# Two more units of a mixture's second product by two Strassen levels, with one set of weight sums

## The chip, the cores and the metric

The kernel runs on one core of one Trainium2 chip. The metric is the device time of one execution in microseconds (us); lower is better. All data are fp32.

## The reference

Linear attention with a decay for each head feeds a mixture of four experts. What is computed, cut to what matters:

```python
# q, k, v: (4, 8, 768, 64); blocks of 64 positions
intra = (qb @ kb.T) * Dmask @ vb
inter = (qb * lam_pow) @ kv_state
kv_state = lam ** 64 * kv_state + (kb * rev_pow).T @ vb
x = attention.transpose(0, 2, 1, 3).reshape(3072, 512)
p = domain_probs / domain_probs.sum(-1)           # (3072, 4)
for e in range(4):                                # w1: (4, 512, 1024), w2: (4, 1024, 512)
    h = maximum(x @ w1[e], 0)
    out += p[:, e:e + 1] * (h @ w2[e])
```

## The kernel before

The 3072 tokens lie in 3 groups g of 1024. A **unit** is one pair (g, e) of group and expert; there are 12. For each unit there is a **first product** (x @ w1, with two Strassen levels: seven outer products M1 to M7, each of seven inner products) and a **second product** (h @ w2). The second product comes in two kinds:

- **One level** (`second_product`, L1071): seven products, each of 4 parts (two token halves by two output halves), each part 4 matmuls of 128x128 by 256. VectorE multiplies each part by the token's gate and adds it to an accumulator (L1089). h is the left operand, so the sums that Strassen needs are formed of h as S sums, and those of w2 as T sums (`prepare_w2`, kept in `w2_sums` in DRAM).
- **Two levels** (`nested_product`, L1370): seven products of seven inner products, 2 matmuls each. w2 is the left operand, in inner operands kept in DRAM (`w2_ops`, made by `prepare_w2_ops` from S sums of w2), and h the right one, with T sums. GpSimd multiplies h by the gate beforehand (`gated`) and forms the inner sums of h (`inner_sums`); VectorE forms the outer sums (`outer_sums`) and adds each inner result to `sums` (seven tiles of the `stage` pool). Results of experts add up there. The result is transposed: group 1's is parked in DRAM, gathered and transposed by VectorE (`first_result`), group 2's is turned at the end.

`NEST` is the index of the first unit of the second kind. Before it is 6: units 0 to 3 are (0, 0) to (0, 3), 4 and 5 are (1, 0) and (1, 1), 6 and 7 are (1, 2) and (1, 3), 8 to 11 are (2, 2), (2, 3), (2, 0), (2, 1). Group 1 so has both kinds: the one-level part of its result goes to DRAM as `partial` and is added on GpSimd when the parked part comes back.

The order is written out by hand. The main loop goes over units `at` and products `i` (7 a unit): an **iteration** does product i of unit `at`'s second product beside product i of unit `at + 1`'s first product. It has 8 **slots** x; slot number is (7 at + i) 8 + x. In each slot a few matmuls are issued, then things from lists: `background` (sums on VectorE), `lately` (attention's VectorE steps), `aside` (GpSimd's gating and inner sums), and `pump`, which starts **chores**. Chores are the steps that prepare weights on GpSimd: load blocks of w1 or w2, form a sum, form one product's inner operands and later store them. `pump` spaces chores by an estimate of GpSimd's time: `tt` adds elements / 480 slots (640 in the two-level stage) to `busy`, and the next chore may begin after PACE times that. A store is queued two slots after the estimated end of its step.

Nearly all DMAs are issued by SyncE (SP in the profile) in program order: a DMA that waits for its data or its buffer holds up all that follow. `feed` loads the next iteration's w1 operands (`ws_in`, 896 KB, two buffers; issued in slot x = 0 of the one-level stage), `feed2` w2 operands two iterations ahead, `feed3` those of the two-level product.

Attention of groups 1 and 2 runs inside the one-level stage, a chunk of 128 tokens at a time: chunk i of group g has its base slot s at BEGIN[g][0] + BEGIN[g][1] i; it loads at s - 10 (`load_more`), and then `turn`, `scores` and `values` follow. Group 2's chunks use a copy of q and k rearranged through DRAM (`across`): 128 small DMAs of 32 KB, 32 for each of the four batches, on the list `pieces`. `trickle` issues one of them in every odd slot; `load_more` first issues all that are left of its batch and earlier ones:

```python
            trickle(sum(b <= where(n)[1] for b, _ in pieces))
            load_across(n)
            load(n, "k")
```

`pair_sums` forms the Strassen sums of two chunks' output on GpSimd and stores them in `x_blocks`; `x_fill` loads them for group 2's (and group 1's) first product at iteration FILL.

Of the kernel before, what the change touches and what calls it, by code (L numbers as in the profile page):

```python
# [12 lines left out]
ALU = mybir.AluOpType  # L13
# [8 lines left out]
def kernel(  # L22
# [30 lines left out]
    nc = tc.nc  # L53
# [47 lines left out]
    def tt(eng, o, a, b, op):  # L101
        eng.tensor_tensor(out=o, in0=a, in1=b, op=op)  # L102
        if eng is nc.gpsimd:
            busy[0] = max(busy[0], now[0]) + math.prod(o.shape[1:]) / (640 if spare else 480)
        else:
            vector(math.prod(o.shape[1:]), PSUM in (a.space, b.space))
# [15 lines left out]
    units = [(g, e) for g in range(NG) for e in ((2, 3, 0, 1) if g == LAST else range(E))]  # L122
    unit_of = {u: x for x, u in enumerate(units)}
    NEST = 2 * E - 2
# [39 lines left out]
    w2_sums = dram.tile([E, 4, P, 2, W], FP32, name="w2_sums")  # L164
# [45 lines left out]
    def inner(eng, what, to, blk, ops, at):  # L210
# [3 lines left out]
        for i, (name, x, y, op) in enumerate(ops):  # L214
            b[name] = s[:, SLOT[name]]
            tt(eng, b[name], b[x], b[y], op)
        store(lambda: (
            nc.sync.dma_start(out=to[:, 0], in_=blk[:, 0, 0:256]),
            nc.sync.dma_start(out=to[:, 1:5], in_=s[:]),
            nc.sync.dma_start(out=to[:, 5:7], in_=blk[:, 1].rearrange("p (a f) -> p a f", a=2)),  # L220
            made.add(what),
        ))

    SLOT = {"S3": 0, "S2": 1, "S1": 2, "S4": 3, "T3": 0, "T2": 1, "T4": 2, "T1": 3}
# [44 lines left out]
    def w2_block(e, uu, i, j):  # L269
        r = uu * W + i * 256  # L270
        return moe_w2[e, r:r + 256, j * DH:(j + 1) * DH].rearrange("(c p) d -> p c d", p=P)

    def prepare_w2(e):
        st = {}

        def block(name, i, j):
            t = stage.tile([P, 2, 2, DH], FP32, name="w2b", tag="st")
            for uu in range(2):
                for c in (slice(0, 1), slice(1, 2)) if e == 0 else (slice(0, 2),):
                    nc.sync.dma_start(out=t[:, uu, c], in_=w2_block(e, uu, i, j)[:, c])  # L280
            st[name] = t

        def total(name, n, a, b, op):
            t = stage.tile([P, 2, 2, DH], FP32, name="w2o", tag="st")
            flat = [x[:].rearrange("p u c d -> p (u c d)") for x in (t, st[a], st[b])]
            halves(*(x[:].rearrange("p u c d -> p u (c d)") for x in (t, st[a], st[b])), op)
            store(lambda: (
                nc.sync.dma_start(out=w2_sums[e, n].rearrange("p u w -> p (u w)"), in_=flat[0]),
                made.add(("w2", e, name)),
            ))  # L290
            st[name] = t

        return [
            lambda: (block("B12", 0, 1), block("B22", 1, 1)), pause(4),
            lambda: block("B11", 0, 0),
            lambda: total("T3", 2, "B22", "B12", ALU.subtract),
            lambda: (block("B21", 1, 0), total("T1", 0, "B12", "B11", ALU.subtract)),
            lambda: total("T2", 1, "B22", "T1", ALU.subtract),
            lambda: total("T4", 3, "B21", "T2", ALU.subtract),
        ]  # L300


# [14 lines left out]
    def prepare_w2_ops(e, eased):  # L317
        st = {}

        def two(name):  # L320
            if eased:
                t = [small(name)[:] for _ in range(2)]
            else:
                t = stage.tile([P, 2, W], FP32, name=name, tag="st")
                t = [t[:, q] for q in range(2)]
            return [x.rearrange("p (c d) -> p c d", c=2) for x in t]

        def block(name, i, j):
            t = st[name] = two("w2b")
            for q in range(2):  # L330
                r = j * W + q * 256
                src = moe_w2[e, r:r + 256, i * DH:(i + 1) * DH]
                nc.sync.dma_start(out=t[q], in_=src.rearrange("(c p) d -> p c d", p=P))

        def total(name, a, b, op):
            t = two("w2o")
            for q in range(2):
                tt(nc.gpsimd, t[q], st[a][q], st[b][q], op)
            st[name] = t

        def ready(m):
            inner_w2(e, m, st[A_OF[m]], two)

        if not eased:
            return weight_steps(block, total, ready)

        def less():
            a, b = st["A11"], st.pop("A21")
            for q in range(2):
                tt(nc.gpsimd, b[q], a[q], b[q], ALU.subtract)  # L350
            st["S3"] = b

        def drop(*names):
            for n in names:
                del st[n]

        return [
            lambda: (block("A21", 1, 0), block("A22", 1, 1)), pause(6),
            lambda: total("S1", "A21", "A22", ALU.add),
            lambda: (ready("M4"), block("A11", 0, 0), drop("A22")), pause(4),  # L360
            less, lambda: ready("M7"), lambda: (ready("M1"), drop("S3")), lambda: ready("M5"),
            lambda: (total("S2", "S1", "A11", ALU.subtract), block("A12", 0, 1)), lambda: ready("M6"),
            lambda: ready("M2"),
            lambda: total("S4", "A12", "S2", ALU.subtract), lambda: ready("M3"),
        ]

    SUM_AT = {"T1": 0, "T2": 1, "T3": 2, "T4": 3}
# [171 lines left out]
    gate_bc = decay[:]  # L539
# [240 lines left out]
    def pair_sums(g, x, o):  # L780

        s = stage.tile([P, 4, 256], FP32, name="to", tag="st")
        (b12, b11), (b22, b21) = ((t[:, 0:256], t[:, 256:512]) for t in o)
        for to, a, b in ((0, b12, b11), (1, b22, s[:, 0]), (2, b22, b12), (3, b21, s[:, 1])):
            tt(nc.gpsimd, s[:, to], a, b, ALU.subtract)
# [3 lines left out]
            nc.sync.dma_start(out=x_blocks[g - 1, :, x, 3:7], in_=s[:]),  # L789
# [4 lines left out]
    BEGIN = {1: (24, 13), 2: (8 * 19, 16)}  # L794
    steps = []

    def attention(g):
# [3 lines left out]

        for i in range(CPG):
# [3 lines left out]
            put(s, lambda n=n: turn(n, ("s0", "s1")))  # L806
            if comes_across(n):
                put(s - 2, lambda n=n: (decayed(n), nat.pop((n, "k"))))
            put(s + (6 if comes_across(n) else 4), lambda n=n: scores(n, ("s0", "s1")))
            put(s + (12 if comes_across(n) else 10), lambda n=n: values(n, ("s0", "s1")))  # L810
            if n == NG * CPG - 1:
                put(s + 17, turn_gates)
        steps.sort(key=lambda s: s[0])

    def forget():
        while lately:
            take(lately, True)
        assert not states
# [5 lines left out]
    hid = {}  # L824
    def operands(key):

        h = hid[key]

        def step():
            t = h["S3"] = h.pop("A21")  # L830
            tt(nc.vector, t[:], h["A11"][:], t[:], ALU.subtract)

        background.append(step)

    def later_operands(g, e, m):

        def step(h, a):
            if m == "M4":
                t = h["S2"] = h.pop("S3")
                tt(nc.vector, t[:], a[:], t[:], ALU.subtract)  # L840
            elif m == "M2":
# [58 lines left out]
    def inner_sums(e, m, behind=False):  # L900
# [6 lines left out]
        def total(name, x, y):  # L907
            while len(blk) < 4:
                take(background if B_OF[m] in SUM_AT else aside, True)
# [843 lines left out]
```

## Time and profile before

| | before |
|---|---|
| time, median of 3 runs | 1161.52 us (1161.19 to 1163.1) |
| the profiled execution: span from first to last instruction | 1164.6 us |
| TensorE (PE) busy | 1149.6 us, 8039 instructions |
| VectorE (DVE) busy | 810.8 us |
| GpSimd (POOL) busy | 748.3 us |
| ScalarE (ACT) busy | 306.2 us |
| granted TensorE clock | 0.998 |
| one-level stage, 90 to 684 us | DMA share 0.80 |
| two-level stage, 684 to 1113 us | DMA share 0.73 |

The page gives the profiled execution no other time than its span. An engine's busy time leaves out DMA issues and waits. PE counts each fp32 matmul as two instructions. In groups of instructions, the columns are busy time, mean ns of one, and idle time before them with what ended it. In stretches, the columns are the stretch, its length, busy time of each engine with its instructions, TensorE's granted clock, DMA share and GB/s. SPq is SyncE's queue. L102 is the helper through which all two-operand steps of VectorE and GpSimd go.

### The profile page before, as it was taken

To read this page: it belongs to the slowest core of one execution; us is meant where nothing else is said; L and a number is where in the kernel's file an instruction comes from. 1 tells how busy PE (TensorE), PEld (TensorE's weight loads), DVE (VectorE), ACT (ScalarE), POOL (GpSimd) and SP (SyncE) were. 2 spreads that over 40 slices of the span, in tenths; PEclk is the share of its full clock that TensorE was granted. 3 is DMA by queue.
4 is the path that set the end of the run, shared out by engine and by line. 5 is a ranking of instruction groups with operands and counts; after the bars stand their busy time and mean duration, and the time that the engine had idled before them with its cause. 6 is when DMAs were issued, how large, how long until landed. Compare 5 with 4: busy or idle time off the path is not lost.

```text
span 1164.6 us, 21683 instructions
## 1 busy us (share of the span) xinstructions
PE 1149.6 (99%) x8039; PEld 997.4 (86%) x8039; DVE 810.8 (70%) x1483; ACT 306.2 (26%) x618; POOL 748.3 (64%) x720
## 2 busy tenths in 40 slices
PE   8899999999999999999999999999999999999998
PEld 7788888888888888888888888888888888888887
DVE  4576896477478757747946775688875677777785
ACT  4312122112201211221221243342343341341232
POOL 2747427456754862243646395897995898995894
PEclk9999999999999999999999999999999999999999
DMA  8883668999999797787969557676668877876542
GB/s 191 213 277 119 182 190 255 311 297 284 314 301 298 258 315 204 205 261 240 291 204 281 187 190 227 213 225 216 212 222 261 244 230 227 277 225 212 172 190 73
DMA packets 291705, 270.63 MB, mean 232 GB/s; under 512 B 139600, under 2 KB 239504, under 8 KB 291600
## 3 DMA queue, kind: packets, MB, share of 16 engines
q1 hardware_dynamic: 278848, 265.36, 74.1%
q10 hardware_dynamic: 12752, 3.89, 1.5%
q8 instruction: 64, 1.05, 0.4%
q14 instruction: 41, 0.34, 0.1%
HBM read 191.55 MB, written 81.82 MB: 235 GB/s over the span
## 4 chain that ended last, share of the span: by engine, by line
PE 93%; DVE 4%; DMA 1%; issue 1%; ACT 0%; ACTq 0%; DVEq 0%
PE pg L1017 39%; PE q L1071 24%; PE pq L1370 19%; PE pM L1473 3%; PE pc L1473 2%; DVE m L102 2%; PE sp L676 1%; PE op L730 1%; DMA ws_in<-w_ops 1%; PE op L748 1%; PE sp L683 1%; DVE sums L102 1%; PE qp L646 1%; PE kp L646 1%; DVE hT L102 0%
## 5 line engine op out<-in xcount | busy, mean ns | idle before, releaser
L1017 PE MATMUL pg<-xs,ws_in 128*128 128x256 f32 x1960 | 472.0, 381 | 2.3 <-DMA ws_in<-w_ops 1.2
L1017 PEld LDWEIGHTS pg<-xs,ws_in 128*128 128x128 f32 x1960 | 369.5, 190 | 56.5 <-DVE m L102 4.6
L102 DVE TENSOR_TENSOR m<-pg,m 128x512 f32<-128x512 f32 x451 | 307.1, 687 | 124.6 <-PE pg L1017 112.8
L1071 PE MATMUL q<-w2t,m 128*128 128x256 f32 x1344 | 318.7, 380 | 0.5 <-DVE m L102 0.5
L1071 PEld LDWEIGHTS q<-w2t,m 128*128 128x128 f32 x1344 | 254.1, 190 | 35.8 <-DVE m L102 1.2
L102 POOL TENSOR_TENSOR m<-m,decay 128x512 f32<-128x512 f32 x96 | 121.0, 1282 | 75.2 <-ACT m L1029 58.0
L1029 ACT ACTIVATE m<-m 128x512 f32<-128x512 f32 x132 | 83.0, 630 | 244.4 <-DVE m L102 241.0
L1370 PE MATMUL pq<-acc,w2t 128*128 128x256 f32 x576 | 141.9, 379 | 0.2 <-DVE sums L102 0.2
L102 DVE TENSOR_TENSOR sums<-pq,sums 128x256 f32<-128x256 f32 x223 | 92.7, 421 | 59.2 <-PE pq L1370 47.8
L1089 DVE SCALAR_TENSOR_TENSOR acc<-q,gate,acc 128x256 f32<-128x256 f32 x136 | 65.4, 481 | 87.5 <-PE q L1071 86.6
L1370 PEld LDWEIGHTS pq<-acc,w2t 128*128 128x128 f32 x576 | 109.2, 190 | 15.7 <-POOL w2o L102 0.5
L102 DVE TENSOR_TENSOR m<-m,m 128x512 f32<-128x512 f32 x136 | 112.9, 830 | 4.2 <-ACT m L1029 4.2
L1025 ACT COPY m<-pg 128x512 f32<-128x512 f32 x88 | 51.5, 585 | 161.7 <-PE pg L1017 158.7
L102 POOL TENSOR_TENSOR acc<-hT,acc 128x512 f32<-128x512 f32 x48 | 61.3, 1276 | 5.2 <-PE pq L1370 1.8
L102 POOL TENSOR_TENSOR to<-xc 128x256 f32<-128x256 f32 x16 | 12.6, 785 | 79.6 <-DVE xc L102 47.1
L102 POOL TENSOR_TENSOR acc<-hT,hT 128x512 f32<-128x512 f32 x48 | 60.7, 1282 | 3.9 <-PE pq L1370 3.9
L1370 PE MATMUL pq<-hT,w2t 128*128 128x256 f32 x240 | 61.6, 379 | 0.0
L102 POOL TENSOR_TENSOR xs<-xs 128x256 f32<-128x256 f32 x40 | 30.4, 761 | 47.0 <-DMA xs<-x_blocks 33.3
L102 POOL TENSOR_TENSOR kn<-kn,decay 128x512 f32<-128x512 f32 x16 | 18.1, 1133 | 63.2 <-PE kp L646 27.6
L949 ACT COPY up<-m 128x512 f32<-128x512 f32 x48 | 27.8, 589 | 101.6 <-DVE m L102 101.4
L881 ACT COPY hp<-m 128x512 f32<-128x512 f32 x72 | 41.6, 589 | 37.5 <-DVE hT L102 20.3
L1370 PEld LDWEIGHTS pq<-hT,w2t 128*128 128x128 f32 x240 | 45.6, 190 | 6.2
(140 smaller groups left out, 1371.0 us busy)
## 6 DMA issues: line engine op xcount, KB each, us to landing
ws_in<-w_ops SPq DMA_DIRECT2D x70, 896.0 KB, 6.9
w2t<-w_ops SPq DMA_DIRECT2D x108, 256.0 KB, 3.7
w2b<-in_moe_w_dram SPq DMA_DIRECT2D x56, 256.0 KB, 6.1
w_ops<-ops SPq DMA_DIRECT2D x28, 512.0 KB, 4.7
w2t<-w_sums SPq DMA_DIRECT2D x48, 256.0 KB, 3.7
w2t<-in_moe_w_dram SPq DMA_DIRECT2D x36, 256.0 KB, 3.9
w_sums<-w2o SPq DMA_DIRECT2D x16, 512.0 KB, 5.4
xs<-x_blocks SPq DMA_DIRECT2D x28, 256.0 KB, 4.5
```

Of the source, the lines that this page charges most:

```text
L102: eng.tensor_tensor(out=o, in0=a, in1=b, op=op)
L646: nc.tensor.transpose(out=x[:, ac * C:(ac + 1) * C], in_=y[:, 2 * ac:2 * ac + 2].rearrange("p r d -> p (r d)"), identity=ident[:],)
L676: nc.tensor.matmul(out=sp[r][half[x], ac * BL:(ac + 1) * BL], lhsT=hc(kT)[half[r], ac, blk[x]], rhs=hc(qT)[half[r], ac, blk[x]], start=(ac ...
L881: nc.scalar.copy(out=there[x][:], in_=blk[at][:])
L949: nc.scalar.copy(out=there[at][:], in_=a[at][:])
L1017: nc.tensor.matmul(out=p[:, j * 256:(j + 1) * 256], lhsT=ws[i][:, j * P:(j + 1) * P], rhs=xs[i], start=(fresh and j == 0), stop=True, skip ...
L1025: nc.scalar.copy(out=new[at][:], in_=p[:])
L1029: nc.scalar.activation(out=new[at][:], in_=new[at][:], func=AF.Relu)
L1071: nc.tensor.matmul(out=p[:, s * DH:(s + 1) * DH], lhsT=h[A_OF[m]][:, c * 256 + s * P:c * 256 + (s + 1) * P], rhs=fed2[g, e, m][uu][:, c], ...
L1089: nc.vector.scalar_tensor_tensor(out=o, in0=x, scalar=w, in1=o, op0=ALU.mult, op1=ALU.add)
L1370: nc.tensor.matmul(out=p[:, 0:256], lhsT=fed3[e, m, x // 2][:, x % 2, c * P:(c + 1) * P], rhs=b[B_OF[i]][:, c * 256:(c + 1) * 256], start= ...
L1473: nc.tensor.matmul(out=p[:, s * 256:(s + 1) * 256], lhsT=a[c][:, f:f + P], rhs=b[:, c, j * 256:(j + 1) * 256], start=(s == 0 and c == 0 an ...
```

## The change

`NEST` becomes 4: group 1's units all take the two-level second product, in the order (1, 2), (1, 3), (1, 0), (1, 1). `partial` goes. The one-level product now takes w2 as the S operand and h as the T operand, so that one set of w2 sums in DRAM (`w2_sums`, S1 to S4) serves both kinds: for experts 2 and 3 `prepare_w2` forms the sums and the inner operands in one pass, for experts 0 and 1 `prepare_w2_ops` later reads the sums back. The T sums of h are formed in the place of operands no longer needed. GpSimd's steps are counted at 640 elements a slot everywhere, with a PACE for each unit. Group 2's attention begins at slot 128 and takes 13 slots a chunk. Gates are turned at slot 12 and broadcast into two tiles of the common pool. The plain blocks of w1 are no longer copied into `w1_ops`: for M1, M2 and M4 `feed` loads three pieces. `pair_sums` uses tiles of the common pool in place of `stage`. The core of the diff:

```diff
-            busy[0] = max(busy[0], now[0]) + math.prod(o.shape[1:]) / (640 if spare else 480)
+            busy[0] = max(busy[0], now[0]) + math.prod(o.shape[1:]) / 640
...
-    units = [(g, e) for g in range(NG) for e in ((2, 3, 0, 1) if g == LAST else range(E))]
+    units = [(g, e) for g in range(NG) for e in ((2, 3, 0, 1) if g else range(E))]
-    NEST = 2 * E - 2
+    NEST = E
...
+        if both:                                   # prepare_w2(e, both=True)
+            return [
+                lambda: block("A11", "A21"), lambda: block("A22"), pause(4),
+                lambda: ready("M1"),
+                lambda: total("S3", "A11", "A21", ALU.subtract), lambda: ready("M7"),
+                lambda: total("S1", "A21", "A22", ALU.add), lambda: ready("M5"),
+                lambda: ready("M4"),
+                lambda: (block("A12"), total("S2", "S1", "A11", ALU.subtract)), lambda: ready("M6"),
+                lambda: ready("M2"),
+                lambda: total("S4", "A12", "S2", ALU.subtract), lambda: ready("M3"),
+            ]
...
+        return [                                   # prepare_w2_ops(e)
+            lambda: fetch(SEQ3[0]), pause(4),
+            *(lambda i=i: (i < 6 and fetch(SEQ3[i + 1]), ready(SEQ3[i])) for i in range(7)),
+        ]
...
-    BEGIN = {1: (24, 13), 2: (8 * 19, 16)}
+    BEGIN = {1: (24, 13), 2: (24 + 8 * 13, 13)}
...
+        def idle(slot):
+            return ("s0", "s1") if slot < NEST * 56 else (("q11", "q12"), ("q01", "q02"))[slot // 8 % 2]
...
+    IN_PLACE = {
+        "T3": ("B22", "B12", ALU.subtract, "B12"), "T2": ("T3", "B11", ALU.add, "B11"),
+        "T1": ("B22", "T2", ALU.subtract, "T3"), "T4": ("B21", "T2", ALU.subtract, "T2"),
+    }
...
-            there[x] = bank(tag, "hp")             # outer_sums
-            nc.scalar.copy(out=there[x][:], in_=blk[at][:])
+            if e > NEST:
+                there[x] = bank(tag, "hp")
+                nc.scalar.copy(out=there[x][:], in_=blk[at][:])
...
-        nc.sync.dma_start(out=ws[:], in_=w1_ops[e, MS.index(m)])     # feed
+        if m in PLAIN_A:                           # M1, M2, M4
+            nc.sync.dma_start(out=ws[:, 0], in_=src[0:P, 0:256])
+            nc.sync.dma_start(out=ws[:, 1:5], in_=of[:, 1:5])
+            nc.sync.dma_start(out=ws[:, 5:7], in_=src[P:2 * P].rearrange("p (a f) -> p a f", a=2))
+        else:
+            nc.sync.dma_start(out=ws[:], in_=of)
...
-    SEQ2 = ("M1", "M7", "M4", "M6", "M2", "M5", "M3")
+    SEQ2 = ("M1", "M7", "M6", "M5", "M4", "M2", "M3")
+    THEN = {"M7": "T2", "M6": "T1", "M5": "T4"}
...
-            tt(nc.gpsimd, t[:], t[:], po[:], ALU.add)                # finish_rows
-            store(lambda: nc.sync.dma_start(out=rows[CPG + n], in_=t[:]))
+            nc.sync.dma_start(out=rows[CPG + n], in_=t[:])
...
-    PACE = 1.0, 1.4, 1.0
+    steps.insert(0, (12, turn_gates))
+    PACE = 1.15, 1.15, 1.4, 1.4, 1.3, 1.3, 1.3, 1.4, 1.0, 1.0, 1.0, 1.0
-            chores.extend(prepare_w2(2) + prepare_w1(3) + prepare_w2(3) + prepare_w1(0))
+            chores.extend(prepare_w1(3) + prepare_w2(2, True) + prepare_w2(3, True) + prepare_w1(0))
         if at == NEST:
+            while chores:
+                pump(force=True)
+            chores.extend(prepare_w2_ops(0) + prepare_w2_ops(1))
...
-                pump(PACE[g])
+                pump(PACE[at])
```

## The prediction

> **What bounds the kernel now.** I read the page's busy times first, then the chain that ended last, the same chain in order of time, busy times by stretch, and last the timeline of SyncE's DMA queue, because that is where the moved work goes.
>
> ```profile
> PE 1149.6 (99%) x8039; PEld 997.4 (86%) x8039; DVE 810.8 (70%) x1483; ACT 306.2 (26%) x618; POOL 748.3 (64%) x720
> PE 93%; DVE 4%; DMA 1%; issue 1%; ACT 0%; ACTq 0%; DVEq 0%
> ```
>
> TensorE is 99% busy and 93% of the chain. Busy could still hide slow matmuls, so I look at the chain in order of time: start, length, what.
>
> ```profile
> 345.11 1.73 PE pg L1017 x8
> 346.84 1.73 PE q L1071 x8
> ...
> 762.57 1.74 PE pq L1370 x8
> ```
>
> Eight matmul instructions take 1.73 us in the first product (L1017), in the one-level second product (L1071) and in the two-level one (L1370): 0.216 us each, whatever the stage. One fp32 matmul is two instructions. Next, stretches: one iteration of a one-level unit without attention, one of a two-level unit, the one-level stage, its dense part, the two-level stage.
>
> ```profile
> 607.70:620.65 12.95, 12.95 (x62) 11.40 (x61) 4.01 (x7) 2.34 (x4) 2.74 (x4) 1.00 0.95 284
> 698.40:710.50 12.10, 12.10 (x57) 10.64 (x56) 6.62 (x12) 5.72 (x12) 7.25 (x9) 1.00 0.72 225
> 90.00:684.00 594.00, 591.88 (x4561) 512.94 (x4560) 413.62 (x720) 114.13 (x236) 315.36 (x339) 1.00 0.80 248
> 209.20:447.60 238.40, 237.77 (x2021) 205.32 (x2023) 162.58 (x284) 42.10 (x89) 142.09 (x154) 1.00 0.95 296
> 684.00:1113.00 429.00, 427.09 (x1971) 373.26 (x1970) 311.23 (x555) 150.34 (x289) 353.81 (x312) 1.00 0.73 227
> ```
>
> TensorE idles 2.1 us in each stage, the granted clock is 1.00, and every other engine has room. So time falls one for one with TensorE instructions, unless something makes it wait. The scarce thing is the one-level stage's DMA: 0.80 busy on average, 0.95 over 238 us.
>
> **What is removed from TensorE.** An iteration of a one-level unit has 4 parts of 4 matmuls, a two-level one 7 products of 2: 32 against 28 instructions. Seven iterations, two units: 56 instructions x 0.216 = 12.1 us. The two iterations above differ by 0.85; 14 x 0.85 = 11.9. I take 12.1. Attention, first products and the last unit keep their matmuls.
>
> **VectorE and GpSimd.** Each changed unit loses 28 gate-and-add steps of 0.481 us (L1089) and gains 28 to 49 sums from PSUM of 0.421: at most +7 us a unit. The two-level stage has VectorE at 311 of 429 us; that room hides it, and if it were gone the 7 us would be TensorE's. GpSimd gains 2 x (16 gatings + 28 inner sums) x 1.28 = 113 us and loses 32 w2 totals of 1.3 to 1.45 (44 us) and 8 additions of 1.27 for the parked rows (10 us): 60 us more, spread over a longer two-level stage where it was 82% busy. Hidden: 44 x 1.28 = 56 us in a unit of 85. Sums of h in place number 16 a unit as before; those in SBUF alone cost 0.83, those with one operand in PSUM 0.68:
>
> ```profile
> L102 DVE TENSOR_TENSOR m<-m,m 128x512 f32<-128x512 f32 x136 | 112.9, 830 | 4.2 <-ACT m L1029 4.2
> L102 DVE TENSOR_TENSOR hT<-hp,m 128x512 f32<-128x512 f32 x48 | 32.8, 682 | 2.0 <-ACT hp L881 2.0
> ```
>
> The first two-level unit no longer copies operands to PSUM (its test is now "over NEST"), so some 24 sums go from 0.68 to 0.83: 3.6 us of VectorE, in a unit that now has attention too. I estimate 28 x 0.48 + 41 x 0.69 + 30 x 0.83 + about 22 us of attention = 89 us of 100. The busiest stretches of before had 90% and lost 0.5 us a 30. I charge 1 us (0 to 4).
> [...]
>
> **GpSimd's steps closer.** A step of 1024 elements was given 1024/480 = 2.1 slots; now 1024/640 x 1.15 = 1.8 (units 0, 1) or 2.2 (units 2, 3). It really takes 4 x 0.76 to 0.84 = 3.2 us, 1.8 slots of 1.78 us. The plan has no slack at 1.15, so stores wait in SyncE's queue for GpSimd and all feeds behind them wait too. The w1 feed is normally issued 13 to 15 us ahead of its first matmul and lands in 6.9, so 7 us of such lateness is free. Charge 0, bound 5. By my addition of the paces the list empties near slot 205 of 224, so the forced emptying at NEST costs 0 (bound 5: all seven staging buffers become sums there).
>
> **DMA squeezed together.** Out of the one-level stage go 14 w1 feeds of 896 KB, 28 w2 feeds, 16 reloads of w2 for its two-level operands and 16 partial rows, and 9 x 3/7 of a w1 store. At the dense stretch's 296 GB/s (3.1 us for 896 KB) that is 43 + 25 + 14 + 7 + 12 = 101 us. Left: 0.80 x 594 - 101 = 374 us; the stage is shorter by 14 iterations of 12.95, 594 - 181 = 413; that is 0.91. The stretch at 0.95 lost 0.6 us in 238, so 1 us here (0 to 8).
>
> **Attention moved.** Group 2's chunks start at slots 128 + 13i instead of 152 + 16i. Each of their steps moves, and one issues many DMAs: loading chunk 21 first empties the list of 128 small copies into "across" for all batches. One copy goes out every odd slot, ten before slot 0. Chunk 21 loads at 152 + 80 - 10 = slot 222 before: 10 + 111 = 121 issued, 7 left. After: 128 + 65 - 10 = 183: 10 + 91 + 1 = 102 issued, 26 left. The queue's timeline at slot 222:
>
> ```profile
> 487.00 1.08 SPq L441 DMA_DIRECT2D across<-in_k_dram  x1
> 490.42 0.35 SPq L1092 DMA_DIRECT2D out_dram<-acc  x1
> 490.82 5.67 SPq L441 DMA_DIRECT2D across<-in_k_dram  x8
> 496.54 0.61 SPq L457 DMA_DIRECT2D qx<-across  x1
> 498.19 0.56 SPq L457 DMA_DIRECT2D kx<-across  x1
> 498.81 1.17 SPq L158 DMA_DIRECT2D kn<-in_k_dram  x2
> 500.01 0.50 SPq L1092 DMA_DIRECT2D out_dram<-acc  x1
> 500.56 0.95 SPq L1052 DMA_DIRECT2D w2t<-w_sums  x2
> 501.56 1.34 SPq L930 DMA_DIRECT2D ws_in<-w_ops  x1
> ```
>
> Eight copies in a row, 0.65 us apart, then qx waits for the last to land, then the queue gets to the next iteration's w1 feed, at 501.56 instead of some 5 us earlier. Its first matmul is at 510.9, so nothing stalled. With 26 copies: 26 x 0.65 = 16.9; qx, kx with their wait 2.2; kn 1.2; two w2 feeds 1.0; the first of the feed's three pieces 0.4 (M2 is now fed in three): 21.7 us after the start. Slot 183 is an iteration's last, so the start is about 1.4 us before the next iteration, and the feed is issued 20.3 us into it. The matmul that needs it comes one iteration of 14.3 and one part of 1.7 later, at 16.0. The piece lands 2.5 to 4.5 us after issue; the second piece is needed 0.9 later. Stall: about 8 us (20.3 + 4.5 - 16.9 = 7.9). The queue runs up to two slots ahead of or behind its place, so 4 to 12. Queued behind it too: chunk 21's qx, on which VectorE's transposes wait, inside the same stall.
> [...]
>
> **Other edits, at nothing.** Dropping 8 partial loads helps the queue at 900 us, where 3 us of stalls lie; moving the gate's turn to slot 12, broadcasting gates into two tiles, and three-piece feeds all lie under feeds with 7 us of slack; if that is gone they cost their own 0.4 to 1 us.
>
> **Sum.** The profiled execution spans 1164.6 us, 3.1 above the median of 1161.5, and the page gives no other time of it. Against the span: -12.1 + 8 + 1 + 1 = -2.1, so 1162.5, which is 1159.4 on the median.
>
> **Rivals.** (a) The burst is absorbed, because the queue is ahead by two slots or more: -12.1 + 1 to 2, 1150 to 1152. For it: by the issue times of its copies the queue ran 1 to 2 slots ahead in quiet iterations. Against: in dense ones it was about 1 behind. (b) Slower: SyncE's queue becomes the bound. It decides once stalls exceed 12.1: the burst at 12, and a stage where the issues, 0.5 us each when DMA is free and 0.83 in the densest iterations, leave each feed a few us late: 5 to 8 more. 1161.5 - 12.1 + 12 + 6 = 1167, to 1172. For it: DMA at 0.91 for the whole stage; against: 0.95 was borne for 238 us. (c) GpSimd cannot keep up and the second product's operands come late: 5 + 5 + 8, near 1167 too; less likely, 82% busy before and no TensorE wait on it over 1.3 us.
>
> **How the numbers follow.** Forecast (stall 4 to 12, 1155 to 1164) 0.45; (a) 0.23; (b) 0.24; (c) 0.08. About 0.2%, 2.3 us, is what a measurement can tell. The forecast's own spread straddles that bound on the faster side: 0.23 of it faster, 0.15 same, 0.07 slower. Together 0.46, 0.15, 0.39. The range takes in (a) to 1149.5 and (b) to 1170.
>
> **What would show it.** Iterations of units 4 and 5 at 12.1 us; 26 copies in a row on SyncE's queue, and right after them the only TensorE gap of several us, ahead of the first product's M2 for unit 4. No such gap, and (a) holds; gaps spread over units 1 to 3 with ws_in or GpSimd as releaser, and (b) or (c). I am wrong altogether if two-level units 4 and 5 run slower than 12.1 an iteration.

## The result and the profile after

The changed kernel takes 1240.91 us (median of four runs, 1239.18 to 1244.31) against 1162.01 us before (1161.19 to 1163.1): a ratio of 1.0675, with a 95% interval of 1.0652 to 1.0698. The prediction said 1159.4 and a range to 1170; it was wrong by 81.5 us, in size and in sign. The profiled execution took 1239.18 us and spans 1237.3, that is 72.7 more than the span of before. The medians lie 78.9 apart: the execution profiled before was a long one (it spans 1164.6, those of the same kernel beside the experiments 1160.3 to 1161.5).

First the same three things as before: busy times, chain, and the clock in 40 slices.

```profile
PE 1158.7 (94%) x7983; PEld 998.1 (81%) x7983; DVE 842.6 (68%) x1525; ACT 316.2 (26%) x638; POOL 826.3 (67%) x768
PEclk9999999999889998799899999999999999999999
PE 77%; DVE 10%; DMA 5%; SPq 4%; POOL 1%; issue 1%; ACT 0%; ACTq 0%; DVEq 0%; POOLq 0%
```

The 56 TensorE instructions are gone (8039 to 7983), yet TensorE is busy 9 us longer, because part of its work ran at a lower clock (the slices with 8 and 7), and its share of the chain fell from 93% to 77%. VectorE, DMA and SyncE's queue (SPq) have taken its place: TensorE waits. Next, busy times by stretch (stretch and its length; busy time of PE, PEld, DVE, ACT and POOL; granted clock; DMA share; GB/s), the first four units of each kernel, and then in the changed one the two units that became two-level. Before:

```profile
90.20:191.40 101.20, 100.25 (x766) 86.85 (x765) 79.09 (x138) 19.38 (x38) 48.67 (x54) 1.00 0.60 181
191.40:296.20 104.80, 104.72 (x966) 90.55 (x965) 70.95 (x130) 21.91 (x48) 62.66 (x67) 1.00 0.93 289
296.20:395.20 99.00, 98.45 (x750) 85.15 (x749) 67.51 (x113) 18.20 (x38) 60.38 (x62) 1.00 0.95 301
395.20:495.00 99.80, 99.80 (x838) 86.29 (x837) 68.42 (x122) 17.08 (x36) 44.36 (x54) 1.00 0.81 244
```

After:

```profile
88.50:193.90 105.40, 100.62 (x766) 86.91 (x766) 83.16 (x138) 19.61 (x39) 58.91 (x60) 1.00 0.58 178
193.90:298.40 104.50, 104.50 (x965) 90.52 (x964) 72.53 (x130) 21.80 (x48) 79.20 (x90) 1.00 0.94 294
298.40:426.20 127.80, 112.36 (x989) 93.97 (x989) 72.52 (x129) 19.44 (x46) 69.26 (x79) 0.93 0.90 269
426.20:573.60 147.40, 110.10 (x902) 92.64 (x901) 76.09 (x131) 17.79 (x40) 86.78 (x92) 0.88 0.71 215
573.60:670.20 96.60, 89.88 (x506) 78.19 (x506) 57.92 (x94) 30.50 (x67) 74.02 (x67) 0.96 0.70 228
670.20:754.90 84.70, 84.70 (x394) 74.41 (x393) 62.62 (x114) 25.56 (x46) 70.40 (x65) 1.00 0.78 248
```

The loss has two places. I count units from 0: unit 2 (the third line) grows by 28.8 us, unit 3 by 47.6, unit 0 by 4.2, unit 1 not at all. The two units that became two-level (4 and 5) fall from 99.6 + 91.7 to 96.6 + 84.7. The second of them, seven iterations, runs at 12.10 each with no gap; the first, which still has attention beside it, takes 13.8.

The worst single place is in unit 3. This is the timeline of SyncE's queue there (start, length, line, what):

```profile
466.46 8.22 SPq L435 DMA_DIRECT2D across<-in_q_dram  x11
474.73 10.40 SPq L435 DMA_DIRECT2D across<-in_k_dram  x16
485.17 0.61 SPq L451 DMA_DIRECT2D qx<-across  x1
...
491.98 0.40 SPq L928 DMA_DIRECT2D ws_in<-in_moe_w_dram  x1
...
493.44 0.64 SPq L788 DMA_DIRECT2D x_blocks<-xc  x1
```

The foreseen burst is there: 27 copies in 18.7 us. But what TensorE waits for longest is the last line, and not the first product's feed (`ws_in`) above it. It is the store of two finished chunks' output, stuck behind the burst. Its SBUF tile is to be used again for a sum of VectorE, and VectorE's timeline shows what that does (the bracket is idle time before, and what ended it):

```profile
499.68 0.69 DVE L102 TENSOR_TENSOR m<-pg,m 128x512 f32<-128x512 f32 x1 [21.55 <-DMA x_blocks<-xc]
```

Attention's state update `kv` stood behind that sum in VectorE's program and ran after it, at 501.88, and TensorE waited for `kv`:

```profile
502.35 0.48 PE L730 MATMUL op<-qs,kv 64*64 64x64 f32 x4 [22.82 <-DVE kv L102]
...
505.16 3.19 PE L1018 MATMUL pg<-xs,ws_in 128*128 128x256 f32 x8
508.19 1.89 PE L1072 MATMUL q<-w2t,m 128*128 128x256 f32 x8
```

A chain through three queues, SyncE's, VectorE's and TensorE's, each innocent by itself. Without the store the feed would still have cost much of it: attention's matmuls take 2.8 us (502.35 to 505.16), so TensorE, idle since 479.5, would have reached the feed's matmuls at 482.3, and the feed's first piece landed at 496.3. That is an estimate of 14 us of gap; the store made it 22.8. The last two lines show a second cost: after the gap eight matmul instructions take 3.19 us in place of 1.89; the granted clock is 0.5 from 483.74 to 507.63 us.

### The profile page after: what moved, and what is told of

Its sections match the earlier page's. It is cut to its first block, busy times and chain, and to the rows that moved or that the text cites. A ratio compares the mean times of both kernels' runs of the same rounds, so it can differ in the third digit from the quotient of the medians.

```text
span 1237.3 us, 21855 instructions
## 1 busy us (share of the span) xinstructions
PE 1158.7 (94%) x7983; PEld 998.1 (81%) x7983; DVE 842.6 (68%) x1525; ACT 316.2 (26%) x638; POOL 826.3 (67%) x768
## 4 chain that ended last, share of the span: by engine, by line
PE 77%; DVE 10%; DMA 5%; SPq 4%; POOL 1%; issue 1%; ACT 0%; ACTq 0%; DVEq 0%; POOLq 0%
PE pg L1018 33%; PE pq L1362 24%; PE q L1072 12%; DVE m L102 4%; PE pM L1464 2%; SPq L435 2%; DVE hT L102 1%; DVE sums L102 1%; DVE xs L102 1%; PE pc L1464 1%; DMA ws_in<-w_ops 1%; PE sp L676 1%; PE op L730 1%; DMA across<-in_k_dram 1%; PE op L748 1%
## 5 line engine op out<-in xcount | busy, mean ns | idle before, releaser
L1018 PE MATMUL pg<-xs,ws_in 128*128 128x256 f32 x1960 | 479.5, 385 | 20.5 <-DMA ws_in<-w_ops 11.5
L102 DVE TENSOR_TENSOR m<-pg,m 128x512 f32<-128x512 f32 x451 | 307.7, 687 | 145.2 <-PE pg L1018 111.2
L102 POOL TENSOR_TENSOR m<-m,gb 128x512 f32<-128x512 f32 x128 | 167.2, 1325 | 97.5 <-ACT m L1030 71.6
L1072 PE MATMUL q<-w2t,m 128*128 128x256 f32 x896 | 220.4, 390 | 5.9 <-DVE m L102 5.9
L1072 PEld LDWEIGHTS q<-w2t,m 128*128 128x128 f32 x896 | 173.5, 195 | 31.9 <-DVE m L102 6.7
L1362 PE MATMUL pq<-acc,w2t 128*128 128x256 f32 x800 | 198.1, 381 | 0.2 <-DVE sums L102 0.2
L102 DVE TENSOR_TENSOR sums<-pq,sums 128x256 f32<-128x256 f32 x321 | 133.0, 420 | 86.1 <-PE pq L1362 74.1
L1362 PEld LDWEIGHTS pq<-acc,w2t 128*128 128x128 f32 x800 | 152.2, 191 | 22.0 <-issue 1.1
L102 DVE TENSOR_TENSOR m<-m,m 128x512 f32<-128x512 f32 x96 | 81.5, 851 | 11.9 <-DMA x_blocks<-xc 6.0
L102 POOL TENSOR_TENSOR xs<-xs 128x256 f32<-128x256 f32 x40 | 31.8, 796 | 67.3 <-DMA xs<-x_blocks 64.5
L1362 PE MATMUL pq<-m,w2t 128*128 128x256 f32 x264 | 69.2, 385 | 1.7 <-DVE xc L102 1.6
L102 POOL TENSOR_TENSOR acc<-m,acc 128x512 f32<-128x512 f32 x44 | 57.0, 1295 | 3.2
L1362 PEld LDWEIGHTS pq<-m,w2t 128*128 128x128 f32 x264 | 50.2, 192 | 10.0 <-ACT xc L769 1.7
```

The costliest lines, as they stand in the source:

```text
L1018: nc.tensor.matmul(out=p[:, j * 256:(j + 1) * 256], lhsT=ws[i][:, j * P:(j + 1) * P], rhs=xs[i], start=(fresh and j == 0), stop=True, skip ...
L1072: nc.tensor.matmul(out=p[:, s * DH:(s + 1) * DH], lhsT=h[at][:, c * 256 + s * P:c * 256 + (s + 1) * P], rhs=fed2[g, e, m][x][:, c], start= ...
L1362: nc.tensor.matmul(out=p[:, 0:256], lhsT=fed3[e, m, x // 2][:, x % 2, c * P:(c + 1) * P], rhs=b[B_OF[i]][:, c * 256:(c + 1) * 256], start= ...
```

## The experiments

Each kernel below was run once with a profile, beside the kernel before on the same chip (1162.1 to 1163.3 there). The four executions of the changed kernel lie 5.1 us apart (0.4%); smaller differences are not read. "Excess" of a unit is its length less 0.216 us for each matmul instruction of the two products; attention's own matmuls and the slower clock are in it. The letters of theories in the quoted expectations differ from group to group.

**e1: the burst spread out.** Unit 0 issues three of the small copies in an odd slot.

```diff
-                    trickle()
+                    trickle(1 if at else 3)
```

> The changed kernel, but three of the small copies into across go out in each odd slot of unit 0 (one later), so that none are left when chunk 21 loads. Theory A (two separate queueing faults on SyncE: the burst of 27 copies in unit 3, and the wait for w2 sums at slot 112): the 23 us gap of TensorE in unit 3 and the half-clock stretch of 24 us behind it go, about 35 us: 1200 to 1210. Rival B (the shortened one-level stage asks more of SyncE and the DMA engines than they can give, and the stalls only move): 1225 or more.

Measured 1213.94, 27 us less, between the two expectations. Unit 3's excess fell from 56.7 to 26.2 us and the 22.8 us gap is gone. Unit 2 stayed (126.9 us).

**e2 and e5: order of the weight work.** The sums of the third expert's w2 ahead of the fourth expert's w1; e2 on the changed kernel, e5 on e1.

```diff
-chores.extend(prepare_w1(3) + prepare_w2(2, True) + prepare_w2(3, True) + prepare_w1(0))
+chores.extend(prepare_w2(2, True) + prepare_w1(3) + prepare_w2(3, True) + prepare_w1(0))
```

> The changed kernel, but w2 of expert 2 is prepared before w1 of expert 3, so that its sums are in DRAM long before unit 2 asks for them. Theory A: the 6.7 us gap at the start of unit 2 and its half-clock stretch go, 8 to 15 us: 1226 to 1233; the burst in unit 3 stays. Rival B: the stalls of unit 2 stay in sum, 1238 to 1245.

> Both edits to the changed kernel: small copies early, and w2 of expert 2 before w1 of expert 3. Theory A: both gains add up, 43 to 50 us: 1190 to 1197, and what is left over 1150 is the crowded stage. Rival B: 1220 or more.

Measured 1240.63 and 1222.83. Both are rival B's times. In e2 unit 2's excess falls from 37.1 to 21.7 and unit 1's rises from 13.8 to 25.7: the stalls only change their unit.

**e4: the kernel before with only group 2's attention moved.**

```diff
-    BEGIN = {1: (24, 13), 2: (8 * 19, 16)}
+    BEGIN = {1: (24, 13), 2: (24 + 8 * 13, 13)}
```

> The kernel before, with one edit: group 2's attention begins at slot 128 and takes 13 slots a chunk. Theory A: the burst of some 27 copies appears here too, with one gap of TensorE of 8 to 23 us and a stretch at half clock behind it: 1175 to 1197. Rival B (only the crowded stage makes the burst harmful): within 5 us of before, 1160 to 1167.

Measured 1181.4, 19 us more than before. SyncE's timeline has the same burst; TensorE's timeline shows one gap, here the wait for the w1 feed that the prediction had named:

```profile
429.32 8.17 SPq L441 DMA_DIRECT2D across<-in_q_dram  x11
437.54 10.92 SPq L441 DMA_DIRECT2D across<-in_k_dram  x16
...
453.10 0.47 SPq L930 DMA_DIRECT2D ws_in<-w_ops  x1
```

```profile
460.16 3.75 PE L1017 MATMUL pg<-xs,ws_in 128*128 128x256 f32 x8 [14.47 <-DMA ws_in<-w_ops]
```

The feed goes out 23.8 us after the burst began and lands 7.1 us later. Unit 3 grew by 18.2 us. (Unit 2 grew by 6.4 and unit 4 fell by 6.3, since attention's matmuls moved from the one to the other.) So one line of the change costs more than the 12 us that the whole change saves.

**e11: the same with the copies spread.**

```diff
-                    trickle()
+                    trickle(2)
```

> The kernel before, with group 2's attention at the changed kernel's earlier slots, but the copies into `across` spread two to each odd slot from the first unit on, so that the burst is gone. Theory B (the burst and what is queued behind it on SyncE was the whole price of the earlier attention in the kernel before, 19.3 us when it was tried alone): 1160 to 1168, with no gap over 5 us in the fourth unit. Rival M (the earlier place itself costs, since it puts the chunk steps beside busier engines): 1174 or more, with gaps ahead of attention's own matmuls in units 4 and 5.

Measured 1180.56, rival M's time, but the gaps are not where M has them. The gap in unit 3 is gone (its excess is 10.2 us, 9.1 before), and ws_in is late in three iterations of units 1 and 2 (gaps of 2.1 to 3.8 us). e4 has the same attention in the same slots and differs in the spreading alone: from e4 to e11 unit 3 falls from 118.0 to 100.9, and units 1 and 2 grow from 104.9 and 105.4 to 113.5 and 112.1. So the copies cost nearly as much where they were spread to, 15 us for 17. That spreading is free was wrong. The transfer time of these two units grew by only 2 to 3 us each, so why the copies cost more there than their transfers stays open.

**e7: the kernel before with only GpSimd's steps closer.**

```diff
-            busy[0] = max(busy[0], now[0]) + math.prod(o.shape[1:]) / (640 if spare else 480)
+            busy[0] = max(busy[0], now[0]) + math.prod(o.shape[1:]) / 640
-    PACE = 1.0, 1.4, 1.0
+    PACE = 1.15, 1.4, 1.0
```

> The kernel before, with GpSimd's steps counted at 640 elements a slot everywhere and a pace of 1.15 in group 0's units (1.4 and 1.0 after), nothing else. If the closer steps by themselves make feeds late (theory C): 1167 or more, with gaps of units 1 to 3 that end on ws_in. If they only add to a queue that something else has filled (theory A and B): within 3 us of before, 1159 to 1165.

Measured 1184.41, 21 us more: two numbers of the planner, and no other work. Unit 1 carries the largest part, 8.5 us (unit 0 has 4.3, unit 8 has 3.8); it grew from 104.8 us at a DMA share of 0.93 to this:

```profile
195.50:308.80 113.30, 107.13 (x965) 92.29 (x964) 72.33 (x130) 21.94 (x48) 75.88 (x80) 0.97 0.95 296
```

Length times share is transfer time: 97.5 us before, 107.6 now. Closer steps pulled stores and loads from later units (units 2 and 3 have 3 and 10 us less) into one that was nearly full.

**e6 and e9: SyncE's issues, and the amount of weight work.** e6 issues the small copies from ScalarE's queue, two to an odd slot; e9 is e1 with the inner operands of the fourth expert's w2 made in the two-level stage.

```diff
-pieces.append((b, lambda to=to, src=src: nc.sync.dma_start(
+pieces.append((b, lambda to=to, src=src: nc.scalar.dma_start(
-                    trickle()
+                    trickle(2)
```

```diff
-chores.extend(prepare_w1(3) + prepare_w2(2, True) + prepare_w2(3, True) + prepare_w1(0))
+chores.extend(prepare_w1(3) + prepare_w2(2, True) + prepare_w2(3) + prepare_w1(0))
-            chores.extend(prepare_w2_ops(0) + prepare_w2_ops(1))
+            chores.extend(prepare_w2_ops(3) + prepare_w2_ops(0) + prepare_w2_ops(1))
```

> The changed kernel, with the 128 small copies into across issued by ScalarE in place of SyncE, two in each odd slot, so that none is left at slot 183. If SyncE's issuing is what units 2 and 3 lack (theory S): better than the run with the early copies on SyncE (1213.9), since some 80 us of issues leave it: 1185 to 1203, stalls of unit 2 below half of their 36 us of excess. If it is the DMA engines or GpSimd: 1208 to 1220.

> The run with the early copies (1213.9), and the inner operands of w2 of expert 3 made in the two-level stage, as those of experts 0 and 1 are, in place of in units 1 to 3: 42 stores, 20 us of DMA and 22 us of GpSimd leave the one-level stage. If that stage is overcommitted (theory B, S): 1190 to 1203. If what is left comes from the order of attention's steps in units 3 and 4 alone: 1208 to 1216.

Measured 1217.28 and 1220.04. In e6 SyncE issues in unit 0 for 32 us in place of e1's 81 and in unit 1 for 51 in place of 87, and nothing is gained: unit 1, with two copies to an odd slot, grows from 106.9 to 113.1 as in e11, whoever issues them. Unit 2's DMA engines are busy 0.99 of its 124 us. In e9 unit 2 stays (126.2 us): SyncE issues 134 DMAs there in place of e1's 162, for 88 us in place of 105, and that gains nothing either. Most of the transfers deferred were unit 3's (89 us of transfer time there become 74; unit 2's 120 become 116), and the two-level stage gets new stalls (10.0 us of excess in unit 6).

**e10: attention's VectorE steps first** (on e1). In and just ahead of the two-level units the slots gave VectorE a background sum first and an attention step only when it fitted.

```diff
-                        rest()
-                        if lately and fits():
+                        if lately:
                             take(lately)
+                        rest()
```

> The run with the early copies (1213.9), and in units 3 and up attention's VectorE steps are taken first in each slot, ahead of the sums, instead of last and only where there is room. Theory L (TensorE's gaps of 1 to 3 us ahead of L676 and L730 in units 3 and 4, each with half-clock time behind it, come from that order): these gaps go, 20 to 30 us: 1184 to 1194. If VectorE is simply full there: they move to the sums, 1206 to 1220.

Measured 1197.47, 16.5 us less than e1, where I expected 20 to 30. The group of attention's matmuls that read `kv`, first in e1, then in e10 (count; busy, mean ns; idle before, and what ended it):

```profile
L730 PE MATMUL op<-qs,kv 64*64 64x64 f32 x704 | 17.1, 230 | 10.5 <-DVE kv L102 10.5
```

```profile
L730 PE MATMUL op<-qs,kv 64*64 64x64 f32 x704 | 15.9, 225 | 0.6 <-DVE kv L102 0.6
```

**e12, e13, e14: pace and order again** (on e10): PACE 1.5 in the first four units; PACE 1.0 in the first two; the sums S3, S1, S2 of one expert ahead of its inner operands.

```diff
-    PACE = 1.15, 1.15, 1.4, 1.4, 1.3, 1.3, 1.3, 1.4, 1.0, 1.0, 1.0, 1.0
+    PACE = 1.5, 1.5, 1.5, 1.5, 1.3, 1.3, 1.3, 1.4, 1.0, 1.0, 1.0, 1.0   (e12)
+    PACE = 1.0, 1.0, 1.4, 1.4, 1.3, 1.3, 1.3, 1.4, 1.0, 1.0, 1.0, 1.0   (e13)
```

```diff
-                lambda: ready("M1"),
-                lambda: total("S3", "A11", "A21", ALU.subtract), lambda: ready("M7"),
-                lambda: total("S1", "A21", "A22", ALU.add), lambda: ready("M5"),
-                lambda: ready("M4"),
-                lambda: (block("A12"), total("S2", "S1", "A11", ALU.subtract)), lambda: ready("M6"),
+                lambda: total("S3", "A11", "A21", ALU.subtract),
+                lambda: total("S1", "A21", "A22", ALU.add),
+                lambda: total("S2", "S1", "A11", ALU.subtract),
+                lambda: ready("M1"), lambda: ready("M7"), lambda: ready("M5"),
+                lambda: (ready("M4"), block("A12")),
+                lambda: ready("M6"),
```

> The last variant (copies spread, attention's VectorE steps first; 1197.5) with GpSimd's steps further apart: a pace of 1.5 in the first four units in place of 1.15, 1.15, 1.4, 1.4. Theory C (the closer steps crowd GpSimd, SyncE and the DMA engines, and so make the third unit's feeds late): 1183 to 1193, and the third unit's excess falls from 36.7 to 20 to 28. Rival L (the sums of w2 of the third expert are behind TensorE, and the feed that needs S2 then forces every step and store that is queued ahead of it onto SyncE): 1203 or more, the third unit's excess 40 or more.

> The opposite: a pace of 1.0 in the first two units in place of 1.15 (1.4 in the next two as it was), so that the sums of the third expert's w2 are made earlier. Rival L: the third unit's excess falls from 36.7 to 18 to 28, and the time to 1180 to 1192, with some of it given back in the first two units. Theory C: 1201 or more, the excess of the first two units grows by more than the third gains.

> The same variant with its pace unchanged, but within one expert's w2 the sums S3, S1, S2 are made and stored ahead of the first inner operands (only the order of GpSimd's steps changes, no volume). Rival L: S2 is stored before it is asked for, nothing is forced, and the third unit's excess falls from 36.7 to 15 to 25: 1178 to 1190. Theory C: no change beyond 4 us, 1193 to 1201, since as many steps and copies lie in the same stretch.

Measured 1235.74, 1198.89 and 1201.91. Slower is much worse: in e12 unit 1 is only 0.76 busy with DMA, and unit 2, to which the work is put off, takes 137.7 us. Faster, or in another order, moves stalls and changes the time by less than 5 us. Neither theory explains unit 2: C fails at e12, and L, which is right there (47.0 us of excess), expected more at e13 and e14 than came (33.9 and 31.2 us of excess, from 36.7). What is common to e6 and e10 to e14 is its DMA share, 0.89 to 0.99 at 105 to 122 us of transfer time, where TensorE has some 103 us of work (e20's busy time in that unit, at the end of this section).

**e16: more to move, and nothing else**, in the kernel before: 14 copies of 512 KB between DRAM tensors in unit 2, issued by ScalarE, waited for by nobody.

```diff
+                if at == 2 and x in (2, 6):
+                    nc.scalar.dma_start(out=spare_copy[2 * i + x // 4], in_=moe_w1[0, 0:512].rearrange("(p a) f -> p (a f)", p=P)[:, 0:1024])
```

> The kernel before, with 14 copies of 512 KB from one DRAM tensor to another added in the third unit, issued on ScalarE's queue, nothing waits for them (7.3 MB). Theory D: 20 to 26 us more of transfer time in that unit, which has 5 us to spare, so it grows from 99.0 to 113 to 125 us with late feeds of ws_in and, with the half clock after them, the time is 1175 to 1195. Rival S: the issues on SyncE are the same, the unit stays under 104 us, the time under 1168.

Measured 1181.76, 19 us more than before. Unit 2 by stretch, and TensorE's timeline:

```profile
295.10:407.30 112.20, 101.76 (x749) 86.83 (x749) 67.75 (x113) 18.20 (x38) 59.55 (x62) 0.95 0.95 307
```

```profile
376.75 3.75 PE L1019 MATMUL pg<-xs,ws_in 128*128 128x256 f32 x8 [7.45 <-DMA ws_in<-w_ops]
```

Unit 2 grew from 99.0 to 112.2 us at the same share of 0.95. 12.5 us more of transfer time gave 13.2 us more of wall time. Unit 2 of the kernel before is already full. The rest of the copies' transfer ran in unit 3, where there was room: its share rose from 0.81 to 0.87, some 9 us of transfers, and it grew by 3.8.

**e15: the same number of copies with less in them** (on e10): the inner operands of the third expert's w2 are stored for 16 of 128 partitions, and the fourth expert's are read in their place.

```diff
+        rows_of = slice(0, 16) if e == 2 else slice(0, P)
-        store(lambda: ([nc.sync.dma_start(out=to[:, x], in_=b[n]) for n, x in at], ...
+        store(lambda: ([nc.sync.dma_start(out=to[rows_of, x], in_=b[n][rows_of]) for n, x in at], ...
...
+        x_e = 3 if x_e == 2 else x_e
+        until(("w2", x_e, m))
```

> The variant e10 (copies spread, attention's VectorE steps first; 1197.5), where the inner operands of w2 of the third expert are stored for 16 of 128 partitions only, by as many copies as before, and the products that read them read the fourth expert's instead (the output is not the reference's). GpSimd's steps, the pace and the number of issues on SyncE stay. Theory D (the DMA engines' time bounds the third unit): some 5.6 MB less to move at 3.2 us per MB, so about 18 us less of transfer time there, the unit falls from 127.4 to 106 to 114 us, the time to 1170 to 1184. Rival S (issues on SyncE and GpSimd's closer steps): the unit stays over 122 us, the time over 1190.

Measured 1191.51. Unit 2 in e10 and in e15:

```profile
304.00:431.40 127.40, 110.79 (x989) 93.04 (x988) 73.27 (x129) 19.45 (x46) 70.42 (x80) 0.93 0.94 294
```

```profile
302.60:419.20 116.60, 104.55 (x989) 88.77 (x989) 73.19 (x129) 19.43 (x46) 71.36 (x80) 1.00 0.88 268
```

10.8 us shorter with SyncE's and GpSimd's steps as they were: for these 10.8 us it was bytes, not issues. It is less than the expected 13 to 21, and the whole is only 6 us better, since unit 3 took 5 back (111.0 us); the time is on rival S's side of its line. With its engines 0.88 busy the unit still takes 116.6 us, so transfers are not all that holds it.

**e17 and e18: a version that stores less** (on e10). The plain blocks among the inner operands of w2, 3 of 7 pieces for the third and fourth expert, are not stored a second time but read where they lie; e18 adds PACE 1.0 in the first two units.

```diff
+        if e in (2, 3):
+            at = tuple(a for a in at if a[0][0] == "S")
...
+                    nc.sync.dma_start(out=o, in_=w2_form(x_e, A_OF[m])[:, 2 * j:2 * j + 2, i * P:(i + 1) * P])
...
-    PACE = 1.15, 1.15, 1.4, 1.4, ...
+    PACE = 1.0, 1.0, 1.4, 1.4, ...   (e18 alone)
```

> The variant e10, where the plain blocks among the inner operands of w2 of the third and fourth expert are not stored a second time (3 of 7 pieces of each operand, 4.6 MB less in the third unit): the two-level units read them from where they are. The result is the reference's. Theory D: about 14 us less of transfer time in the third unit, which falls from 127.4 to 110 to 117 us; the two-level units read in more and smaller pieces, 0 to 6 us; time 1176 to 1190. Rival S: 31 copies fewer on SyncE of 164 are worth at most 5 us in that unit, 1191 to 1200.

> e17 with a pace of 1.0 in the first two units (1.15 before), which moves about 1.5 MB of transfers from the third unit into the first, where the DMA engines are 0.66 busy. Theory D: 2 to 8 us below e17, 1170 to 1186. Rival S (closer steps cost): 3 us or more above e17.

Measured 1185.4, 12 us less than e10, with unit 2 at 116.6 us as in e15; and 1182.42, too close to e17 to be read.

**e19 and e20: T4 first.** In e18 TensorE still waits 3.3 us twice, ahead of the second product's fifth step, in units 0 and 2. The first of the two:

```profile
148.42 1.19 PE L1074 MATMUL q<-w2t,m 128*128 128x256 f32 x4 [3.25 <-DVE m L102]
```

Here the operand is the in-place sum T4, whose four steps were queued behind sums of the first product. e19 puts them in front, in the order in which they are read; e20 adds fewer copies in unit 0 and a pace between.

```diff
+        if name == "T4":
+            background[0:0] = [lambda at=at: step(at) for at in ("12", "22", "11", "21")]
...
-                    trickle(1 if at else 3)
+                    trickle(1 if at else 2)   (e20 alone)
-    PACE = 1.0, 1.0, 1.4, 1.4, ...
+    PACE = 1.1, 1.0, 1.3, 1.4, ...   (e20 alone)
```

> e18 with the four in-place steps of T4 ahead of the first product's sums in VectorE's list, in the order in which the second product reads them. Theory Q (the order of VectorE's queue makes the two gaps of 3.4 and 3.5 us in the fifth steps of units one and three): both gaps fall under 1 us, and with the half clock after them the time falls by 6 to 12 us, to 1170 to 1177. Rival V (VectorE has too much to do in that stretch, so what is put first delays the PSUM banks of the first product instead): the gaps move to matmuls of the first product, 1179 to 1186.

> e19 with two copies into `across` to an odd slot of the first unit (three before), and a pace of 1.1, 1.0, 1.3, 1.4 in the first four units (1.0, 1.0, 1.4, 1.4 before), so that the third chunk's load of k in the first unit's last step is not behind so much on SyncE. If that load's gap of 3.9 us goes and nothing is late later: 4 to 8 us below e19. If the transfers that leave the first unit come back as late feeds in the second or third, where the DMA engines are over 0.9 busy: within 4 us of e19 or above it.

Measured 1174.94 and 1171.02. In e19 the group of one-level second products has no idle time left (6.6 us in e18), and unit 2 falls from 111.2 to 105.7 us. e20 is too close to e19 to be read; its first four units:

```profile
88.50:190.20 101.70, 100.53 (x766) 86.97 (x766) 82.36 (x138) 19.64 (x39) 59.36 (x61) 1.00 0.65 190
190.20:299.50 109.30, 107.12 (x965) 91.37 (x964) 73.66 (x130) 21.79 (x48) 84.82 (x97) 0.98 0.93 291
299.50:405.10 105.60, 103.42 (x990) 89.05 (x989) 71.55 (x129) 19.59 (x46) 69.27 (x76) 1.00 0.96 293
405.10:511.40 106.30, 102.15 (x902) 87.18 (x900) 76.04 (x133) 17.80 (x40) 82.52 (x88) 1.00 0.86 262
```

70 of the 79 us are back. The version still loses to the kernel before (1163.3 beside it), and no kernel tried beats that.

## Why the prediction was wrong, step by step

**The saving was right.** 12.1 us for 56 instructions: a dense two-level iteration takes 12.10 us, and unit 5 84.70, seven of them. Unit 4, at 13.8 an iteration, does show the prediction's last sign of being wrong: 6.7 us of waits, 3.4 us of the slower clock and attention's own matmuls are in its time.

**"Attention moved": 8 us (4 to 12); it was 17 alone and 27 in the whole.** The mechanism was right, and 26 copies were 27. In e4 the term, gap and slower clock together, measures 14.5 + 2.6 us. The parts that were too small: each copy took 0.71 us in place of 0.65, and the feed, there in one piece, landed 7.1 us after its issue where I allowed 4.5. In the changed kernel the feed went out 25.5 us after the burst began, 21.7 in my sum, and the victim was another. I followed what stands behind the burst only as far as loads (the feed, qx, kx), and not to the store of `x_blocks`, whose tile VectorE waits for. Taking the burst away (e1) gave 27 us. In e4 the store of `x_blocks` was late too, and VectorE's sums did not wait for it; what in the change brought that tile's reuse forward was not tried.

**"DMA squeezed together": 1 us (0 to 8); in unit 2 alone it was over 10.** The sum itself was good: 374 us of transfers for the one-level stage, and the four lines above make 105.4 x 0.58 + 104.5 x 0.94 + 127.8 x 0.90 + 147.4 x 0.71 = 379. What failed is the step from there to "0.91 on average, and 0.95 was borne". Unit 0 uses 61 us of its 105; unit 2 needs 115 in a unit that TensorE would finish in about 103. The 0.95 of before was borne, still under 1; e16 shows that the next 12 us in that unit count one for one. Divided by unit, the sum would have read over 100% in unit 2. Of the 28.8 us there, 10.8 go with the bytes alone (e15, and e17 again), and 22.2 are gone in e20, where the order of T4 and the pace are changed too.

**"GpSimd's steps closer": 0 (bound 5); it was 21 in the kernel before.** I asked whether GpSimd keeps up, and it does: one wait of TensorE of over 0.5 us ends on it in the changed kernel, 0.99 us. I did not ask what its earlier steps trigger: their stores and loads moved into a unit whose DMA engines were already 0.93 busy (e7). How much of the 79 us is this term can't be told apart from the one above, since both are in the same DMA share (0.94 in unit 1, 0.90 in unit 2).

**"VectorE": 1 us (0 to 4); it was some 24.** The busy time left room, as I said (76.1 us in unit 3 and 57.9 in unit 4, under the 89 that I had estimated; over the whole it grew by 31.8, where my terms make some 18). The order was not looked at: 16.5 us for attention behind background sums in units 3 and 4 (e10), 7.5 for T4 behind sums of the first product (e19). I priced the in-place sums as work and not as a wait with things queued in front of it.

**The clock: no term; it was 17.7 us.** No row that I had read of before shows a lower one, so none could price it. By the clock's records 17.7 us of TensorE's time went to it in the changed kernel, and 66.0 to gaps of over 0.5 us, against 0 and 3.2 before. Together that is 80.5 us; the main loop's excess grew by 84.3, and 84.3 less the 12.1 saved is 72.2, the spans' difference within 0.5. Of the 66.0, 29.6 end on `kv`, 12.9 on VectorE's sums `m` and 12.9 on the w1 feed.

Rival (b) had the sign and a cause near the right one, a full transport with feeds late in units 1 to 3, at 1167 to 1172; it named SyncE's issues as the bound, and fewer of them gained nothing in units 0 and 1 (e6) and in unit 2 (e9). Rival (c), GpSimd too slow, has only the 0.99 us to show. All rivals fell short: none had a chain from the burst through VectorE, a unit over 100%, or the clock.

What stays open: e20's last 8 us against before, to which the saved 12 should be added. Its trace has 14.4 us of gaps over 0.5 us, behind late feeds in units 1 and 2 (4.1) and behind VectorE (10.3), and 1.7 us of slower clock; they were not tried apart, and some 7 of the 20 are in neither. Of unit 2's 28.8 us, what neither the bytes nor T4's order explains was not tried apart either.

## What to carry to other kernels

Divide the transfer time by stage and not over the whole: here a unit at 0.93 to 0.95 had no room, and what was pulled into it came back as wall time, be it bytes (e16), a planner's faster pace (e7) or copies spread out of a burst (e11). When something is put in front on a queue that runs in program order (here 18.7 us of copies on SyncE's), follow everything behind it, stores too, to the buffer that each store frees and to the engine that waits for that buffer. And price a moved sum by what is in its engine's queue at that moment, not by its duration (here T4's place was worth 7.5 us, e19).

## What the runs showed of the hardware

Gaps of TensorE cost more than their length in these runs. By the clock's records the granted clock of the changed kernel fell to 0.5 in eight stretches of the main loop, of 3.41, 6.83 and 23.89 us; they begin whole multiples of 3.41 us apart (the first three at 323.31, 364.27 and 381.34 us). At its two gaps of over 6 us (6.5 us from 317.96 and 22.8 us from 479.53) the stretch began 5.4 and 4.2 us into the gap and reached 5.7 and 5.3 us past its end: 2.8 us lost after the first, 2.4 after the second. After the 14.5 us gap of e4 the first sixteen matmul instructions took 6.08 us (460.16 to 466.24) in place of 3.46: 2.6 lost. So over these three gaps the loss did not grow with the length. The changed kernel lost 17.7 us in the eight stretches, seven at gaps of over 2 us and one at two gaps of 1.8 and 0.8 us. A gap of 2.6 us did it (from 378.71), and gaps of 3.3 us (the changed kernel, from 144.38) and 3.9 us (e15, at 359 us, in a unit with a granted clock of 1.00) did not: by these runs the length of a short gap does not decide it. What does is not shown.
